# A linear-attention and two-layer MLP kernel: 256-token seven-product form for the second layer's first chunk, states' and score products in array quarters, two warm-up products fewer

## The chip, the core and the metric

One core of a Trainium2 chip runs the whole program. The metric is the time of one execution on the device, in microseconds (us), as the median of several runs; less is better. The core has a matrix engine (PE, with its weight loads listed as PEld), a vector engine (DVE), an activation engine (ACT), a third elementwise engine (POOL), and DMA queues that SP issues here. Matrix products are written to eight banks of an accumulation memory (`ps`), 128 partitions by 512 float32 each.

## What is computed

Linear attention with a decay per head, in blocks of the sequence, and then two MLP layers. Cut to what matters:

```
intra = (q k^T * Dmask) v                        per block, Dmask = lam^(i-j), lower triangle
inter = (q * lam^(pos+1)) state                  the states' product
state = lam^block * state + (k * lam^(rest))^T v
x     = intra + inter                            1536 tokens x 512 (2 batches, 8 heads of 64)
h     = x @ w_in    (512 x 2048);  g = elu(h);           x = g @ w_out    layer 1
h     = x @ w_in2   (512 x 2048);  g = max(h,0) + alpha*min(h,0);  out = g @ w_out2
```

Inputs and results are float32 (the weights float64, read as pairs of words).

## The kernel before

**Precision.** For the MLP each float32 operand is split into a high and a low part (names end in `h` and `l`), and a product of two operands is three matmuls: high x high, high x low, low x high (`for w, x in ((0, 0), (0, 1), (1, 0))`). The attention's products are plain float32; each of their matmuls shows as two records in the trace.

**Attention.** 768 positions are cut into six units of 128, for two batches. A unit has: scores (`scores`, L618: per batch and pair of heads one matmul for each head, on 64 rows of the array, 128 columns of weights), masked by DVE; outputs (`outputs`, L693, on 64-column halves of the array); the update of the state (`state`, L660, 64-column halves; its sum stays in bank 6, is copied to `st` by `new_states`, L412/L414, and decayed in place by ACT, L681); and the states' product (`earlier`, L713: per batch four full 128x128 matmuls with a state tile that has two heads on its diagonal and zeros elsewhere). POOL multiplies keys and queries by powers of the decay (`scale`, L637, L644). Units 0 and 1 make chunk 1 of the tokens (512 of them), 2 and 3 chunk 2, 4 and 5 chunk 0. Key/query blocks (0.5 MB each) and value blocks come through SP's queue in order, four units ahead, then units 4 and 5 behind the first weights.

**MLP.** Each layer has eight steps j; a step handles 256 of the 2048 hidden features as two tiles q. Chunks t = 1 and 2 are taken together: `seven` (L894) forms the four quarter blocks of their up products with seven products in place of eight (a Strassen-like scheme: `PRODUCTS` names the weight part, the token part and the sum that each goes to), six matmuls of 512 columns each. Copies of the bank on ACT (`kept`) and adds on DVE (`tile`, L908) form the other sums between the products; the sums of token blocks (T1 to T4) are made once per layer by `combine` and `combine_parts`, the sums of weights (S1 to S4) each step. Chunk 0, the first chunk, is `plain` (L862): per tile twelve matmuls of 512 columns, four contraction blocks times three. `finish` (L807, L818 to L824, L412, L420) activates a tile out of its bank by way of a buffer `rt` (three in turn) into a buffer `g` (eight in turn, `gfree`), split into high and low. `down` (L959) multiplies two `g` tiles with the down weights, six matmuls per 128 outputs, and DVE adds them to `acc` (L971). Weights are converted from words to float32 by ACT and DVE (L446 to L454) and split.

**What sets the order.** No instruction is issued where the code writes it. `Plan` collects operations with estimated costs, buffers read and written and a latency `LAT`, works out when each is needed, and simulates the engines in several rounds (`ROUNDS`); the best round's order is issued, engine by engine. On PE a change of the array's tiling (`mode`: full, rows, cols) costs `CHANGE` in the plan; `STAY`, `SPARE`, `EASE` and `HOLD` are thresholds of its choices. On the chip each engine then runs its own list in order, and semaphores hold it where an operand is not there.

**The start.** `begin` runs three warm-up matmuls (L602), the small products that spread the decays over partitions, and three more, before the first scores.

Of the kernel before, what the change touches and what calls it, by code (L numbers as in the profile page):

```python
# [15 lines left out]
C = 128  # L16
# [40 lines left out]
class Plan:  # L57
# [5 lines left out]
    SPARE = 5.0  # L63
    EASE = 0.3
    HOLD = 2.0
    ROUNDS = 6
    FETCH = 45.0
    AHEAD = 384.0
    STAY = 2.0
    CHANGE = 0.2  # L70
    ENGINES = ("PE", "SP", "ACT", "DVE", "POOL")
# [48 lines left out]
    def simulate(self, first, back=False, log=None):  # L120
# [11 lines left out]
        stock, seen, mode = self.AHEAD, 0.0, None  # L132
# [12 lines left out]
        def begin(e, op):  # L145
            nonlocal dma, stock, seen, mode
            cost = op.costs[e]
            if e == "PE":
                cost += self.CHANGE * (op.mode != mode)
                mode = op.mode  # L150
# [28 lines left out]
        while done < len(self.ops):  # L179
            for e in self.ENGINES:  # L180
# [12 lines left out]
                while ready[e]:  # L193
# [7 lines left out]
                    if e == "POOL" and any(  # L201
# [4 lines left out]
                        continue  # L206
                    slow = op.costs[e] - op.least
# [8 lines left out]
                for item in held:  # L216
                    heapq.heappush(ready[e], item)
            now = events[0][0]
# [11 lines left out]
    def run(self):  # L230
# [4 lines left out]
        first, best = self.needs(), None  # L235
        for _ in range(self.ROUNDS):
            log = []
            begun, end = self.simulate(first, log=log)
            if best is None or end < best[0]:
                best = end, log  # L240
            begun, end = self.simulate({op: -t for op, t in begun.items()}, True)
            first = {op: -t - op.least - op.late for op, t in begun.items()}
# [21 lines left out]
def attention_two_layers(  # L264
# [27 lines left out]
    warm = sb("warm", [128])  # L292
    anti = sb("anti", [C])
    lams_sb = sb("lams_sb", [H + NP])
    lam_sb, lamp = lams_sb[:, 0:H], lams_sb[:, H:H + NP]
    last_key = sb("last_key", [64])
    row = mem.tile([1, 128 + H], F32, tag="row", name="row")
    fill = sb("fill", [32])

    pair_acc = sb("acc", [2, 4, CH])  # L300
# [20 lines left out]
    rts = sb("rt", [3, CH])  # L321
# [10 lines left out]
    def x0(p):  # L332
        return later_tile(("x0", p), f"x0{'hl'[p]}", [NCC, CH], F32R, f"x0{p}")

# [20 lines left out]
    st = low[:, 2:4].rearrange("p b (a i) -> p b a i", a=NP)  # L355
    top = sb("qpsm", [3, 512], F32, "ut")
    qp = top[:, 0].rearrange("p (a i) -> p a i", a=NP)
    lamc = qp[:, :, C - 1:C]
# [13 lines left out]
    b_quad.update({("T4", p, o): b_quad["B12", p, o] for p in range(2) for o in range(2)})  # L372
    b_x0 = {(p, o): Buf() for p in range(2) for o in range(4)}
# [7 lines left out]
    b_rt = [Buf() for _ in range(3)]  # L381
# [49 lines left out]
    def convert(l, j, part):  # L431
# [16 lines left out]
        op({"DVE": vec2(1024)}, lambda e: nc.vector.tensor_scalar(  # L448
# [75 lines left out]

    late = []

    def combine_parts(o):

        cols = slice(o * 256, (o + 1) * 256)

# [643 lines left out]
```

## Time and profile before

| what | value |
|---|---|
| median of 3 runs | 557.79 us (557.32 to 558.06) |
| the profiled execution | 558.09 us, of which span 556.3 us |
| PE busy | 550.7 us, 99% |
| DVE, POOL, ACT busy | 69%, 58%, 53% |
| HBM read, written | 45.62 MB, 3.15 MB |

How to read it: the profile covers one execution, from its first to its last instruction (the span). An engine is busy while one of its instructions runs; matmuls overlap, so the steps from start to start tell PE's speed, and a matmul's own duration (0.39 us for 512 columns) includes its way through the array. A chain of waits follows the last instruction back to what released it, step by step.

### The profile page before, as it was taken

The page shows a single profiled execution, that of the slowest core. Times are in us where ns is not written, and L with a number is a line of the kernel's source. Part 1 is how long each engine was busy: PE and PEld are TensorE (multiplying, and loading weights), DVE is VectorE, ACT ScalarE, POOL GpSimd, SP SyncE. Part 2 cuts the span into 40 slices and gives each one's busy share as a digit, 9 for nine tenths or more (in the row PEclk, how much of TensorE's full clock was granted, in tenths as well). Part 3 has the DMA queues.
Part 4 walks back from the last instruction along what each step waited for, and adds up shares of the span by engine and source line. Part 5 has one row for each costly group of instructions (what it writes and reads, how often), then busy time and mean ns, then how long its engine had stood idle before and what let it go on. Part 6 is the DMA issues. An engine that isn't in the chain of part 4 may idle for free.

```text
span 556.3 us, 7398 instructions
## 1 busy us (share of the span) xinstructions
PE 550.7 (99%) x2872; PEld 458.3 (82%) x2872; DVE 383.8 (69%) x499; ACT 294.0 (53%) x470; POOL 324.4 (58%) x226
## 2 busy tenths in 40 slices
PE   9999999999999999999999999999999999999997
PEld 7888888888888888888888888888888888888886
DVE  5689688797676757577856964649676757674554
ACT  3586775757475646557645646644454535434220
POOL 4655742556769474928459679477666583927020
DMA  8992222201404222221310120132222222000114
GB/s 326 402 368 80 77 75 77 75 18 59 153 0 152 75 77 75 75 77 49 133 47 1 75 77 1 46 106 77 75 77 75 77 75 77 0 1 0 39 38 151
DMA packets 18308, 49.23 MB, mean 88 GB/s; under 512 B 1250, under 2 KB 1506, under 8 KB 18274
## 3 DMA queue, kind: packets, MB, share of 16 engines
q1 hardware_dynamic: 18272, 48.77, 25.2%
q8 instruction: 22, 0.36, 0.3%
q14 instruction: 12, 0.10, 0.1%
q10 hardware_dynamic: 2, 0.00, 0.0%
HBM read 45.62 MB, written 3.15 MB: 88 GB/s over the span
## 4 chain that ended last, share of the span: by engine, by line
PE 97%; ACT 1%; DVE 1%; issue 0%; ACTq 0%
PE ps L959 47%; PE ps L894 24%; PE ps L862 20%; PE ps L618 2%; PE ps L693 2%; PE ps L713 2%; PE ps L660 1%; PE ps L602 1%; ACT kd L634 0%; ACT dmst L412 0%; DVE dmst L414 0%; DVE qpsm L624 0%; ACT qbh L412 0%; ACT wt L446 0%; ACT ps L681 0%
## 5 line engine op out<-in xcount | busy, mean ns | idle before, releaser
L971 DVE TENSOR_TENSOR acc<-ps,acc 128x512 f32<-128x512 f32 (+1 forms) x169 | 115.9, 687 | 93.1 <-PE ps L959 91.9
L420 POOL TENSOR_TENSOR g<-rt,g 128x512 fp32r<-128x512 f32 x83 | 120.4, 1457 | 80.5 <-ACT g L412 78.2
L959 PE MATMUL ps<-wdh,g 128*128 128x512 f32 (+1 forms) x388 | 118.4, 387 | 0.0
L959 PE MATMUL ps<-g,wdh 128*128 128x512 f32 x384 | 118.1, 389 | 0.0
L807 ACT ACTIVATE rt<-ps 128x512 f32<-128x512 f32 x96 | 57.3, 598 | 95.7 <-DVE ps L908 55.9
L959 PEld LDWEIGHTS ps<-wdh,g 128*128 128x128 f32 x388 | 72.6, 188 | 14.9
L959 PEld LDWEIGHTS ps<-g,wdh 128*128 128x128 f32 x384 | 72.1, 188 | 14.9
L412 ACT CAST g<-rt 128x512 fp32r<-128x512 f32 x96 | 59.3, 620 | 38.9 <-DVE rt L824 25.2
L959 PE MATMUL ps<-wdl,g 128*128 128x512 f32 (+1 forms) x194 | 75.0, 387 | 0.0
L959 PE MATMUL ps<-g,wdl 128*128 128x512 f32 x192 | 74.7, 389 | 0.0
L420 POOL TENSOR_TENSOR wsl<-wt,wsh 128x1024 fp32r<-128x1024 f32 x12 | 29.4, 2449 | 47.8 <-ACT wsh L412 29.9
L824 DVE SCALAR_TENSOR_TENSOR rt<-rt,beta,ps 128x512 f32<-128x512 f32 x48 | 35.6, 742 | 25.9 <-ACT rt L807 25.9
L420 POOL TENSOR_TENSOR wt<-wt 128x256 f32<-128x256 f32 x54 | 42.4, 796 | 12.5 <-DVE wt L454 5.9
L420 POOL TENSOR_TENSOR wdl<-wt,wdh 128x1024 fp32r<-128x1024 f32 x14 | 38.1, 2723 | 19.5 <-ACT wdh L412 19.3
L454 DVE SCALAR_TENSOR_TENSOR wt<-raw,wt 128x1024 uint32<-128x1024 uint32 x32 | 46.0, 1436 | 0.0
L908 DVE TENSOR_TENSOR ps<-ps,ut 128x512 f32<-128x512 f32 x42 | 29.3, 698 | 21.9 <-PE ps L894 21.8
L959 PEld LDWEIGHTS ps<-wdl,g 128*128 128x128 f32 x194 | 36.4, 188 | 7.4
L412 ACT COPY ut<-ps 128x512 f32<-128x512 f32 x42 | 24.6, 589 | 33.5 <-PE ps L894 33.4
L959 PEld LDWEIGHTS ps<-g,wdl 128*128 128x128 f32 x192 | 36.0, 188 | 7.6
L451 DVE SCALAR_TENSOR_TENSOR wt<-raw,wt 128x1024 uint32<-128x1024 uint32 x32 | 42.0, 1316 | 0.2
L446 ACT ACTIVATE wt<-raw 128x1024 f32<-128x1024 f32 x32 | 36.6, 1143 | 4.7 <-POOL wt L420 3.1
L862 PE MATMUL ps<-x0l,wah 128*128 128x512 f32 x128 | 38.8, 389 | 0.0
(127 smaller groups left out, 932.9 us busy)
## 6 DMA issues: line engine op xcount, KB each, us to landing
raw<-in_w1i SPq DMA_DIRECT2D x8, 1024.0 KB, 5.5
raw<-in_w1o SPq DMA_DIRECT2D x8, 1024.0 KB, 4.9
raw<-in_w2i SPq DMA_DIRECT2D x8, 1024.0 KB, 5.6
raw<-in_w2o SPq DMA_DIRECT2D x8, 1024.0 KB, 4.8
blk<-in_kqT SPq DMA_DIRECT2D x12, 512.0 KB, 11.5
blk<-in_vk SPq DMA_DIRECT2D x10, 512.0 KB, 11.5
out<-acc SPq DMA_DIRECT2D x11, 256.0 KB, 2.0
blk<-in_vk SPq DMA_DIRECT2D x2, 256.0 KB, 9.4
```

Source lines behind the costliest of these rows:

```text
L412: nc.scalar.copy(dst(), src())
L420: lambda e: on(e).tensor_tensor(out=dst(), in0=a(), in1=b(), op=alu),
L446: op({"ACT": 1.14}, lambda e: nc.scalar.mul(t, upper.bitcast(F32), 2.0 ** -112), [b_r], [b_t])
L451: op({"DVE": vec(1024)}, lambda e: nc.vector.scalar_tensor_tensor(out=tu, in0=lower, scalar=29, in1=tu, op0=ALU.logical_shift_right, op1=A ...
L454: op({"DVE": vec(1024)}, lambda e: nc.vector.scalar_tensor_tensor(out=tu, in0=upper, scalar=0x80000000, in1=tu, op0=ALU.bitwise_and, op1=A ...
L807: op({"ACT": act(512, True)}, lambda e: nc.scalar.activation(rt(i), h(), AF.Relu, scale=-1.0), [b_h], [b_r])
L824: op({"DVE": vec(512) + 0.06}, lambda e: nc.vector.scalar_tensor_tensor(out=rt(i), in0=rt(i), scalar=beta[:, f:f + 1], in1=h(), op0=ALU.mu ...
L862: nc.tensor.matmul(out=banks[k], lhsT=wa(s, w)[:, cc, q * 128:(q + 1) * 128], rhs=(both[t][x] if t else x0(x))[:, cc, :], start=i == 0, st ...
L894: nc.tensor.matmul(out=banks[k], lhsT=left(s, a, w)[:, cc, :], rhs=quad(b, x)[:, cc, :], start=bool(opens and i == 0), stop=bool(closes an ...
L908: op({"DVE": vec(512)}, lambda e: nc.vector.tensor_tensor(out=banks[to], in0=banks[k], in1=ut(u), op=ALU.add), [b_ps[k], b_ut[u]], [b_ps[to]])
L959: nc.tensor.matmul(out=p_, lhsT=lhs, rhs=rhs, start=i == 0, stop=i == 5)
L971: op({"DVE": vec(w)}, lambda _, a=a, p_=p_: nc.vector.tensor_tensor(out=a(), in0=p_, in1=a(), op=ALU.add), [b_ps[k], *b_a], b_a)
```

## The change

- **First chunk, second layer.** From step j = 2 on (`FIRST = [8, 2]`: never in the first layer) the up products of chunk 0 are made by `seven_halves`: its 512 tokens are two halves of 256, which take the places of chunks 1 and 2 in the seven-product scheme, with six matmuls of 256 columns per product. The four sums share two banks by halves. `combine_halves` makes the sums T1 to T4 of the halves once, at the beginning of the layer; they live in two former `g` buffers and a new one, so `gfree` has six, and `rt` two.
- **Quarters.** Scores and states' product run on 64x64 quarters of the array. The state holds 64x64 blocks without the zeros, for batch 1 with the two halves of the partitions exchanged (`rows`), so that one product of 16 matmuls serves both batches, alternating over the quarters. The queries of batch 1 are multiplied in two halves, to exchange them; DVE may do it too. The state is copied in one piece, and decayed per batch and pair with a power from a small copy (`last`).
- **Warm-up.** One matmul in place of three behind the decays' products.
- **Plan.** Other thresholds, four rounds, doubled PE costs in the first 6.5 us, higher costs of the weight conversion's DVE steps.

```diff
-    SPARE = 5.0
-    EASE = 0.3
-    HOLD = 2.0
-    ROUNDS = 6
+    ROUNDS = 4
...
+    RULES = [(4.0, 5.0, 0.3, -1.0)]
...
-    rts = sb("rt", [3, CH])
+    rts = sb("rt", [RT, CH])
...
+        if m in ("T1", "T2", "T3"):
+            i = int(m[1])
+            tag = f"g{5 + i}" if i < 3 else "qh3"
+            return later_tile(("qh", i), "qh", [2, 2, CH // 2], F32R, tag)[:, p]
+        c, o = {"B11": (0, 0), "B21": (1, 0), "B22": (1, 1), "T4": (0, 1), "B12": (0, 1)}[m]
+        return x0(p)[:, 2 * c:2 * c + 2, o * 256:(o + 1) * 256]
...
+            self.rows = [half(hs ^ b) for hs in range(2)]
...
                 for pr in range(NP):
-                    for hs in range(2):
+                    for hs, s in ((0, 0), (1, 1), (0, 1), (1, 0)):
                         nc.tensor.matmul(
-                            out=banks[ks[hs]][:, pr * C:(pr + 1) * C],
-                            lhsT=x.kq[half(hs), 0, pr, :], rhs=x.kq[half(hs), 1, pr, :],
-                            start=True, stop=True)
-            pe(0.89, run, [x.b_kq], [b_ps[k] for k in ks], 32, "rows")
+                            out=banks[ks[hs]][half(s), pr * C:(pr + 1) * C],
+                            lhsT=x.kq[half(hs), 0, pr, half(s)],
+                            rhs=x.kq[half(hs), 1, pr, :], start=True, stop=True)
+            pe(0.86, run, [x.b_kq], [b_ps[k] for k in ks], 64, "quarters")
...
+            pe(0.86, run, [b_st, *b_qs[m % 2]], [b_ps[k] for k in ks], 64, "quarters")
...
-        plan.behind(pe(0.4, spread, [b_row, b_one], [b_ps[k]]), run_up(3))
+        plan.behind(pe(0.4, spread, [b_row, b_one], [b_ps[k]]), run_up(1))
...
-    gfree = [4, 5, 6, 7, 0, 1, 2, 3]
+    gfree = [4, 5, 0, 1, 2, 3]
...
+    def seven_halves(l, j):
+        s = j % 2
+        ka, kb = 3 + j % 2, 4 - j % 2
+        left_, right_ = slice(0, 256), slice(256, 512)
+        home = {0: (kb, left_), 1: (ka, left_), 2: (ka, right_), 3: (kb, right_)}
...
+                        nc.tensor.matmul(
+                            out=at(k), lhsT=left(s, a, w)[:, cc, :], rhs=halved(b, x)[:, cc, :],
...
+            def kept(u, k=k):
+                copy(lambda: ut(u)[:, left_], lambda: at(k), [b_p[k]], [b_ut[u]], 256, True)
...
+            if b == "B11":
+                kept(0)
+            elif b == "B21":
+                tile(0, 1)
+            elif b == "T1":
+                kept(1)
+            elif b == "T2":
+                kept(2)
+            elif b == "B22":
+                tile(2, 2)
+                finish(l, 2 * j, lambda: banks[ka], [b_p[1], b_p[2]], (l, j, 0, 0), True)
+            elif b == "T3":
+                tile(1, 3)
+            else:
+                finish(l, 2 * j + 1, lambda: banks[kb], [b_p[0], b_p[3]], (l, j, 1, 0), True)
...
             else:
+                combine_halves(1)
                 merge((), downs(1, 0, T0))
...
-                            plain(l, j + 1)),
+                            first(l, j + 1)),
```

The new states' product, with the loops that set the order of the quarters:

```python
for pr in range(NP):
    for hs in range(2):
        for b, x in enumerate(units[m]):
            nc.tensor.matmul(
                out=banks[ks[b]][half(hs), pr * C:(pr + 1) * C],
                lhsT=st[x.rows[hs], b, pr, :],
                rhs=qss[m % 2][x.rows[hs], b, pr * C:(pr + 1) * C],
                start=False, stop=True, skip_group_check=True)
```

What moves on PE around the end of the attention, from the states' product of unit 3 on. Before (L618 scores, L713 states' product, L693 outputs, L660 state, L862 the first up product, tile by tile):

```order
L618 MATMUL ps<-blk 128x128 x8
L713 MATMUL ps<-qs,dmst 128x128 x4
L693 MATMUL ps<-sm,blk 64x128 x8
L618 MATMUL ps<-blk 128x128 x8
L862 MATMUL ps<-qbh,wah 128x512 x4
L862 MATMUL ps<-qbl,wah 128x512 x4
L862 MATMUL ps<-qbh,wal 128x512 x4
L660 MATMUL ps<-blk,kd 64x64 x16
L693 MATMUL ps<-sm,blk 64x128 x8
L618 MATMUL ps<-blk 128x128 x8
L713 MATMUL ps<-qs,dmst 128x128 x8
```

And of the change (L671 scores, L768 states' product, L748 outputs, L721 state, L927 up product):

```order
L671 MATMUL ps<-blk 64x128 x32
L768 MATMUL ps<-qs,dmst 64x128 x16
L671 MATMUL ps<-blk 64x128 x32
L927 MATMUL ps<-qbh,wah 128x512 x4
L927 MATMUL ps<-qbl,wah 128x512 x4
L927 MATMUL ps<-qbh,wal 128x512 x4
L748 MATMUL ps<-sm,blk 64x128 x16
L721 MATMUL ps<-blk,kd 64x64 x16
L768 MATMUL ps<-qs,dmst 64x128 x16
```

Both batches' scores of unit 5 now stand ahead of the first up product (before, those of its second batch stood behind it), and both batches' states' product of unit 4 is one group.

The first chunk's up products in the second layer, on PE, before (`ps_80` and `ps_81` are banks 3 and 4, `ps_82` to `ps_84` the banks of the down products):

```order
L862 MATMUL ps_80<-x0h_108,wah_503 128x512 x4
L862 MATMUL ps_80<-x0l_109,wah_503 128x512 x2
L959 MATMUL ps_82<-wdh_589,g3_845 128x512 x2
L959 MATMUL ps_82<-wdl_599,g3_845 128x512
L959 MATMUL ps_82<-wdh_589,g0_727 128x512 x2
L959 MATMUL ps_82<-wdl_599,g0_727 128x512
L862 MATMUL ps_80<-x0l_109,wah_503 128x512 x2
L862 MATMUL ps_80<-x0h_108,wal_516 128x512 x4
```

And of the change, at step j = 6 (`ps_78` and `ps_79` are banks 3 and 4; `qh_2375`, `qh_2425` and `qh_2414` hold T1, T2 and T3 of the halves):

```order
L1013 MATMUL ps_78<-qh_2375,wsh_933 128x256 x4
L1013 MATMUL ps_78<-qh_2375,wsl_1006 128x256 x2
L1013 MATMUL ps_79<-qh_2425,wsh_933 128x256 x4
L1013 MATMUL ps_79<-qh_2425,wsl_1006 128x256 x2
L1013 MATMUL ps_78<-x0h_106,wsh_933 128x256 x2
L1013 MATMUL ps_78<-x0l_107,wsh_933 128x256 x2
L1013 MATMUL ps_78<-x0h_106,wsl_1006 128x256 x2
L1013 MATMUL ps_79<-qh_2414,wsh_933 128x256 x4
L1013 MATMUL ps_79<-qh_2414,wsl_1006 128x256 x2
```

Four products of 256 columns follow each other directly; the third adds to the bank half that the first wrote, the fourth to that of the second, and a copy by ACT (`kept`) reads each half in between.

## Rows read from the trace of the kernel before

**Rows 1.** The page: busy time by engine, and the chain that ended last, by engine.

```profile
PE 550.7 (99%) x2872; PEld 458.3 (82%) x2872; DVE 383.8 (69%) x499; ACT 294.0 (53%) x470; POOL 324.4 (58%) x226
...
PE 97%; ACT 1%; DVE 1%; issue 0%; ACTq 0%
```

**Rows 2.** Stretches: us; busy PE, PEld, DVE, ACT, POOL; granted clock, DMA share, GB/s.

```profile
27.80:40.48 12.68, 11.88 (x190) 10.60 (x189) 10.15 (x13) 11.13 (x26) 6.06 (x5) 1.00 1.00 377
...
54.93:553.20 498.27, 498.27 (x2205) 412.43 (x2203) 342.83 (x438) 260.84 (x394) 294.62 (x197) 1.00 0.19 65
```

**Rows 3.** The chain in order of time: start, us, what; one first chunk (L862).

```profile
102.81 5.44 PE ps L862 x24
```

**Rows 4.** Timeline of PE and weight loads at the end, 256 columns: start, us, instruction.

```profile
551.62 0.40 PE L959 MATMUL ps<-wdh,g 128*128 128x256 f32 x2
...
552.58 0.31 PEld L959 LDWEIGHTS ps<-wdh,g 128*128 128x128 f32 x2
...
552.93 0.28 PE L959 MATMUL ps<-wdl,g 128*128 128x256 f32 x1
```

**Rows 5.** Timeline of PE in the attention.

```profile
3.59 1.65 PE L602 MATMUL ps<-warm 128*128 128x128 f32 x6
5.17 3.79 PE L618 MATMUL ps<-blk 64*128 64x128 f32 x32
...
23.38 2.06 PE L618 MATMUL ps<-blk 64*128 64x128 f32 x32
25.37 1.97 PE L693 MATMUL ps<-sm,blk 128*64 128x128 f32 x32
27.27 2.05 PE L713 MATMUL ps<-qs,dmst 128*128 128x128 f32 x16
29.25 1.15 PE L660 MATMUL ps<-blk,kd 128*64 128x64 f32 x32
30.23 1.05 PE L693 MATMUL ps<-qpsm,blk 128*64 128x128 f32 x16
...
40.48 1.19 PE L862 MATMUL ps<-qbh,wah 128*128 128x512 f32 x4
...
43.44 1.15 PE L660 MATMUL ps<-blk,kd 128*64 128x64 f32 x32
...
45.40 1.16 PE L618 MATMUL ps<-blk 64*128 64x128 f32 x16
46.49 2.05 PE L713 MATMUL ps<-qs,dmst 128*128 128x128 f32 x16
48.30 1.18 PE L862 MATMUL ps<-qbh,wah 128*128 128x512 f32 x4
...
51.23 1.09 PE L693 MATMUL ps<-qpsm,blk 128*64 128x128 f32 x16
...
53.13 2.05 PE L713 MATMUL ps<-qs,dmst 128*128 128x128 f32 x16
54.93 1.17 PE L862 MATMUL ps<-qbh,wah 128*128 128x512 f32 x4
```

**Rows 6.** Timeline of POOL and DVE there: unit 5's queries, the up weights' low part.

```profile
38.07 3.51 POOL L644 TENSOR_TENSOR qs<-blk,qpsm 128x512 f32<-128x512 f32 x2 [0.22 <-DMA blk<-in_kqT]
...
38.95 1.48 DVE L420 TENSOR_TENSOR wal<-wt,wah 128x1024 fp32r<-128x1024 f32 x1
```

**Rows 7.** Timeline in the second layer: a product's end on PE and its copy on ACT.

```profile
431.49 0.62 PE L894 MATMUL ps<-qT2h,wsl 128*128 128x512 f32 x2
...
432.14 0.59 ACT L412 COPY ut<-ps 128x512 f32<-128x512 f32 x1 [1.61 <-PE ps L894]
```

**Rows 8.** Groups by line and shape on ACT: count, busy us, mean ns, idle before.

```profile
L446 ACT ACTIVATE wt<-raw 128x1024 f32<-128x1024 f32 x32 | 36.6, 1143 | 4.7 <-POOL wt L420 3.1 <-DMA raw<-in_w2i 0.8 <-DMA raw<-in_w1o 0.4
...
L412 ACT COPY ut<-ps 128x512 f32<-128x512 f32 x42 | 24.6, 589 | 33.5 <-PE ps L894 33.4
...
L783 ACT ACTIVATE qpsm<-ps,lams_sb 128x128 f32<-128x128 f32 x4 | 1.1, 369 | 7.3 <-PE ps L787 7.3
```

More of the change, by code (lines that the diff above doesn't have):

```diff
@@ L148, in begin @@
             if e == "PE":
+                if now < self.COLD and not back:
+                    cost *= 2
                 cost += self.CHANGE * (op.mode != mode)
@@ L234, in run @@
                 a.before.append(op)
[L235 to L242, printed above, removed]
+        best = None
+        for self.STAY, self.SPARE, self.EASE, self.HOLD in self.RULES:
+            first = self.needs()
+            for _ in range(self.ROUNDS):
+                log = []
+                begun, end = self.simulate(first, log=log)
+                if best is None or end < best[0]:
+                    best = end, log
+                begun, end = self.simulate({op: -t for op, t in begun.items()}, True)
+                first = {op: -t - op.least - op.late for op, t in begun.items()}
         for e, op in best[1]:
@@ L291, in attention_two_layers @@
     beta = sb("beta", [2 * NU])
-    warm = sb("warm", [128])
-    anti = sb("anti", [C])
+    early = sb("early", [2, CH], F32, "qh3").rearrange("p a b -> p (a b)")
+    warm, anti = early[:, 0:128], early[:, 128:256]
+    last_key, fill = early[:, 256:320], early[:, 320:352]
+    row = early[0:1, 384:512 + H]
     lams_sb = sb("lams_sb", [H + NP])
[L295 to L298, printed above, removed]
+    lam_sb, lamp = lams_sb[:, 0:H], lams_sb[:, H:]
+    last = [sb(f"last{b}", [NP]) for b in range(B)]
+    RT = 2
     pair_acc = sb("acc", [2, 4, CH])
@@ L380, in attention_two_layers @@
     b_ut = [Buf() for _ in range(3)]
-    b_rt = [Buf() for _ in range(3)]
+    b_rt = [Buf() for _ in range(RT)]
     b_ps = [Buf() for _ in range(8)]
@@ L779, in masks @@
                     data1=anti, initial=0.0, op0=ALU.mult, op1=ALU.add)
-        def powers(e):
-            for pr in range(NP):
-                nc.scalar.mul(qp[:, pr], p2[:, pr * C:(pr + 1) * C], lamp[:, pr:pr + 1])
+        for hs in range(2):
+            op({"DVE": 1.3}, lambda e, hs=hs: masks(e, hs), [b_lam, b_anti], [b_dm[hs]], True)
+        k = turn("ps", 8)
+        p2 = banks[k]
         def last_row():
@@ L984, in merge @@
         while True:
+            while not gfree and next(dn, None):
+                pass
             a, b = next(up, None), next(dn, None)
```

237 lines of the change are left out of this document (155 added, 82 removed).

## The prediction

> **What bounds the kernel.** I read the page's shares first, then the chain of waits, then the stretches, then the timeline of PE. PE is busy 99% of the span and carries 97% of the chain that ended last [rows 1]; DVE at 69% and ACT at 53% hold 1% of it each, POOL at 58% nothing. The stretches divide the span in two. From 54.93 to 553.20 us PE is busy for all of 498.27 us [rows 2]. A 512-column product takes 5.44 / 24 = 0.2267 us there [rows 3]; of the kernel's 2214 such matmuls 24 stand ahead of 54.93, and 2190 x 0.2267 + 12 x 0.12 (the narrow ones at the end) = 497.9 us. That is the stretch, so nothing stalls in it, and only fewer or faster matmuls, or a new stall, change its length. Ahead of it lies the attention. Up to 40.48 us the DMA engines are full (share 1.00, 377 GB/s [rows 2]), and POOL waits for key and query blocks as they land: the first of unit 5 at 38.07 [rows 6]. So there two limits lie close together.
>
> **Part 1: the first chunk's up products in the second layer.** A chunk was 24 matmuls of 512 columns, 5.44 us [rows 3]. It becomes seven products of six matmuls of 256 columns. The trace has that width at its end: from 551.62 to 552.93 lie 11 steps, 0.119 us each; the weight loads, 0.31 us for two that overlap, run without a gap beside them [rows 4]. So 42 x 0.12 = 5.04 us, 0.40 us less. The loop takes this form for j = 2 to 7, six chunks: **-2.4 us**. Where PE is the bound throughout, this counts in full, if the order causes no stall.
>
> What it adds elsewhere: per chunk three ACT copies and three DVE adds of 256 columns, and once four sums and four splits of the chunk (16 operations of DVE, POOL and ACT). The new halves are first read after the whole second j = 1 stage; DVE, POOL and ACT have 31, 42 and 47% of the span free for them [rows 1]. I cost them at nothing; were their cover gone, the 12 subtractions among them are the largest part.
>
> The wait it adds: products pass through ACT copies before the same half bank is added to again. In the order eight times only one product of 0.72 us (6 x 0.12) stands between. What has to fit: in the trace a product's last issue at 431.49 + 0.45 ends its slot at 431.94, and the copy starts at 432.14, 0.20 later [rows 7]. A 256-column copy lies between 369 ns (128 columns) and 589 ns (512) [rows 8], 0.44 by a straight line. With 0.05 for the way back that is 0.69 against 0.72. So the wait is nil if ACT is free, and up to 1.14 us if a weight conversion (1143 ns [rows 8]) has just begun; behind the waiting matmul all of PE is queued. ACT is idle about half the time [rows 1], so I am near the lower end: 0.1 us each, **+0.8 us** (bounds 0 and 8 x 1.14 = 9.1).
>
> Two resources shrink: six buffers for activated tiles instead of eight, two for results in work instead of three. In PE's new order the shortest time from a buffer's last reader to its next is five products, 5 x 6 x 0.2267 = 6.8 us (before: nine, 12.2), and it must hold a cast and a split. I cost both at nothing; a stall would fall on PE at full price.
>
> **Part 2: the attention in quarters.** A record of the state product in two column tiles costs (30.23 - 29.25) / 32 = 0.0306 us; two score products of 16 records cost 1.99, a single one between other modes 45.40 to 46.49 = 1.09 [rows 5]. So a second block costs 0.90, and changing the array's mode 0.19. No row shows a quarter tile. If four run at once, a product of 32 records costs no less than 0.98 (the fastest record there is); if only two do, 32 x 0.0563 = 1.80. Both halves, rows (scores) and columns (states), do show two at once, so I take 0.98. Then a states' product of both batches falls from 1.80 (46.49 to 48.30 [rows 5]) to 0.98, five times; a score block goes from 0.90 to 0.98, twelve times, the first unit's two at the slow rate of the start.
>
> What lies on the path? PE's order puts both score blocks of unit 5 ahead of the first up product. At 377 GB/s a block of 0.52 MB takes 1.4 us, so their second key block lands near 39.4, its scores end near 40.4, and the first up product starts where it did, at 40.48. The weights for it are no earlier bound (their last DVE step ended at 38.95 + 1.48 = 40.43 [rows 6]). From there the trace needs 14.45 us to 54.93 [rows 5]. After: up 2.96 (40.48 to 43.44), outputs 1.90, state 0.98, states' product 0.98 + 0.17 for the change, up 2.93 (48.30 to 51.23), outputs 1.90, states' product 1.15 = 12.97. **-1.5 us.** Ahead of 40.48 about 3.3 us of PE work go as well (three states' products -2.5, nine changes of mode -1.7, four warm-up records -1.05, the moved score block +1.0, slower scores 11 x 0.08 = +0.9); they turn into waiting for unit 5. The two warm-up matmuls are 4 of the 6 records of 1.58 us [rows 5], all inside this slack; that the scores then start earlier and still at the slow rate (3.79 / 32 = 0.118 us a record, against 0.062 in the later pair [rows 5]) costs nothing there. Bounds of the part: +1.6 if two tiles run at once in the two late states' products alone, and 1.3 us more gain if the last key block lands with the first.
>
> The queries' products become 15 for 10, 13 on POOL, at up to 3.51 / 2 = 1.76 us each [rows 6]; the last reader, unit 5's states' product, stands 11.8 us behind the first up product, so they are hidden. The state is copied in one piece for two, and ACT's three small copies run once, at the start. I cost these at nothing.
>
> A rule of the Trainium skill speaks against this part: the page TensorEngine Tiling (Array Packing), section Restrictions and Gotchas, says that different row tiles can't use one PSUM bank at the same time. In the new states' product each batch has one bank, and both row halves write it. The scores' pair at 1.99 us [rows 5] shows two row tiles at once on separate banks; no run here shows them on one. By the rule the product would run two tiles at a time, and the sum be 556.3 in place of 554.7; it is the first rival.
>
> **Sum.** -2.4 + 0.8 - 1.5 = -3.1 us on the profiled execution's 558.09 us (span 556.3 and 1.8 around it) = 555.0; that execution lies 0.3 above the median 557.79, so the forecast is **554.7 us** on the median's scale. What a measurement can tell here is about 0.2%, 1.1 us.
>
> **Rivals.** *One bank, two tiles* (11%): states' products cost 1.80. The three early ones (+2.5) still fit into the 3.3 us of slack; the two late ones take back 2 x 0.82. 557.79 - 2.4 + 0.8 - 1.5 + 1.6 = 556.3. For it: no row shows otherwise; against it: different partitions of the bank are written.
> *The short cover in the halves* (16%): each of the eight waits meets half a weight conversion, 0.57 us, or the fewer buffers stall PE as much. +4.6 for +0.8: 558.5. For it: conversions stand right ahead of some of these copies in ACT's order; against: ACT follows PE without one stall now. The part breaks even at 0.3 us a wait.
> *Quarters run two at a time everywhere* (8%), the slower side: ten later score blocks +8.2 (0.82 each), the first unit's +3.6 (64 records at 0.118 for 32), states' products +4.1, less the 3.3 of slack and the 1.5: +11.1 in place of -1.5, so 557.79 - 2.4 + 0.8 + 11.1 = 567.3. It decides from 0.041 us a record on, where 620 records (the slow ones counted by their price) use up the slack and both gains. For it: no row of quarters; against: each half already gives the factor two, and weight loads of two tiles overlap.
> *The last key block lands early* (13%): attention 1.3 better and no waits in the halves: 552.6.
> That the halves don't run at 0.12 would need 0.13 a matmul to lose the gain; with rows 4 I give it no chance of its own.
>
> **How the numbers follow.** Forecast 52%, with its own range 553.3 to 556.2. Faster by over 0.2% (under 556.7): forecast 51, early block 13, one bank 7, a little of the short cover 1: 0.72. Slower (over 558.9): quarters 8 and a quarter of the short cover 4: 0.12. The rest, 0.16, is no change. The range goes down to 552.0, under the early block, and up to 558.6, past the short cover's time; beyond lie the quarters above and little below.
>
> **What would show it.** The halves: 42 matmuls of 256 columns per chunk at 0.12 steps, and PE idle ahead of them, released by the copy on ACT: 0.8 us in all if I am right, over 3 if the short cover holds. Quarters: 32 records of scores in 0.98 us after the first unit, and of states in 0.98 (1.80 by the rule on banks). Waiting of PE between 36 and 40 us that ends with scores of unit 5; first up product near 40.5, the unbroken stretch from about 53.4. Wrong would be a stall of PE in the first layer or at the change of layers, or an up product that starts well ahead of 40 us.

## The result: 0.9% slower

The changed kernel takes **562.64 us** (median of 5 runs, 562.1 to 563.14) against 557.75 us of the kernel before, run beside it: ratio 1.0087, 95% interval 1.0073 to 1.0100. I had predicted 554.7 us, in a range of 552.0 to 558.6. Of the 7.9 us between forecast and time, nearly all was lost in the first 80 us, where the prediction had costed new things at nothing.

### The profile page after: what moved, and what is told of

It reads as the page before. It is cut to its first block, busy times and chain, and to the rows that moved or that the text cites. A ratio compares the mean times of both kernels' runs of the same rounds, so it can differ in the third digit from the quotient of the medians.

```text
span 560.7 us, 8291 instructions
## 1 busy us (share of the span) xinstructions
PE 546.8 (98%) x3248; PEld 458.5 (82%) x3248; DVE 427.2 (76%) x565; ACT 305.3 (54%) x530; POOL 277.6 (50%) x187
## 4 chain that ended last, share of the span: by engine, by line
PE 92%; ACT 3%; DVE 2%; DMA 1%; issue 1%; SPq 0%; ACTq 0%
PE ps L1086 47%; PE ps L959 24%; PE ps L927 12%; PE ps L1013 5%; PE ps L748 2%; DMA blk<-in_kqT 1%; PE ps L671 1%; ACT ps L736 1%; PE ps L721 1%; PE ps L768 1%; ACT kd L687 1%; DVE ut L438 0%; ACT qbh L430 0%; DVE g L438 0%; SPq L418 0%
## 5 line engine op out<-in xcount | busy, mean ns | idle before, releaser
L1098 DVE TENSOR_TENSOR acc<-ps,acc 128x512 f32<-128x512 f32 (+1 forms) x169 | 115.0, 684 | 63.0 <-PE ps L1086 61.6
L438 POOL TENSOR_TENSOR g<-rt,g 128x512 fp32r<-128x512 f32 x62 | 91.3, 1473 | 102.9 <-ACT g L430 92.2
L1086 PE MATMUL ps<-g,wdh 128*128 128x512 f32 x384 | 118.6, 390 | 2.8 <-DVE acc L432 2.8
L1086 PE MATMUL ps<-wdh,g 128*128 128x512 f32 (+1 forms) x388 | 118.9, 388 | 0.0
L1086 PEld LDWEIGHTS ps<-g,wdh 128*128 128x128 f32 x384 | 72.2, 188 | 18.2 <-DVE acc L432 3.2
L1086 PEld LDWEIGHTS ps<-wdh,g 128*128 128x128 f32 x388 | 71.6, 188 | 14.2 <-DVE acc L1098 0.3
L1086 PE MATMUL ps<-wdl,g 128*128 128x512 f32 (+1 forms) x194 | 75.1, 387 | 0.0
L1086 PE MATMUL ps<-g,wdl 128*128 128x512 f32 x192 | 74.9, 390 | 0.0
L430 ACT COPY ut<-ps 128x512 f32<-128x512 f32 (+1 forms) x60 | 31.4, 523 | 63.4 <-PE ps L959 44.6
L438 POOL TENSOR_TENSOR wal<-wt,wah 128x1024 fp32r<-128x1024 f32 x13 | 31.3, 2405 | 49.8 <-ACT wah L430 39.2
L884 DVE SCALAR_TENSOR_TENSOR rt<-rt,ps 128x512 f32<-128x512 f32 x48 | 32.2, 682 | 16.6 <-ACT rt L882 15.9
L1086 PEld LDWEIGHTS ps<-wdl,g 128*128 128x128 f32 x194 | 36.4, 188 | 7.6
L1086 PEld LDWEIGHTS ps<-g,wdl 128*128 128x128 f32 x192 | 36.1, 188 | 7.5
L438 POOL TENSOR_TENSOR wsl<-wt,wsh 128x1024 fp32r<-128x1024 f32 x12 | 34.3, 2856 | 15.7 <-ACT wsh L430 11.5
L438 POOL TENSOR_TENSOR wt<-wt 128x256 f32<-128x256 f32 x42 | 34.2, 831 | 13.5 <-DVE wdl L438 8.9
L438 DVE TENSOR_TENSOR g<-rt,g 128x512 fp32r<-128x512 f32 x34 | 37.4, 1108 | 4.5 <-ACT g L430 4.1
L438 POOL TENSOR_TENSOR wdl<-wt,wdh 128x1024 fp32r<-128x1024 f32 x10 | 24.7, 2472 | 31.7 <-ACT wdh L430 31.6
```

The source lines that it names most:

```text
L430: nc.scalar.copy(dst(), src())
L438: lambda e: on(e).tensor_tensor(out=dst(), in0=a(), in1=b(), op=alu),
L884: op({"DVE": vec(512)}, lambda e: nc.vector.scalar_tensor_tensor(out=rt(i), in0=rt(i), scalar=-1.0, in1=h(), op0=ALU.add, op1=ALU.max), [b ...
L1086: nc.tensor.matmul(out=p_, lhsT=lhs, rhs=rhs, start=i == 0, stop=i == 5)
L1098: op({"DVE": vec(w)}, lambda _, a=a, p_=p_: nc.vector.tensor_tensor(out=a(), in0=p_, in1=a(), op=ALU.add), [b_ps[k], *b_a], b_a)
```

## The profile after

First the page: busy time, the granted clock in 40 slices, the transfers of instructions, and the chain by engine.

```profile
span 560.7 us, 8291 instructions
PE 546.8 (98%) x3248; PEld 458.5 (82%) x3248; DVE 427.2 (76%) x565; ACT 305.3 (54%) x530; POOL 277.6 (50%) x187
...
PEclk8989989999999999999999999999999999999999
...
q8 instruction: 25, 0.41, 0.3%
...
PE 92%; ACT 3%; DVE 2%; DMA 1%; issue 1%; SPq 0%; ACTq 0%
```

PE has 3.9 us less to do than before [rows 1], and yet the span is 4.4 us longer (556.3 before): PE now idles, and in three of the first six slices its granted clock shows 8 tenths and not 9. "issue" holds 1% of the chain, where it held 0 [rows 1]. Second, PE's waits: engine, line, what released it, us in total, times, longest.

```profile
PE ps L1086 <- DVE acc L432: 2.8, 1, 2.8
PE ps L748 <- DVE qbl L787: 2.1, 2, 1.4
PE ps L671 <- DMA blk<-in_kqT: 2.0, 1, 2.0
PE ps L721 <- issue: 1.3, 1, 1.3
...
PE ps L721 <- ACT ps L736: 1.0, 1, 1.0
```

None of them is in the kernel before. Third, PE's timeline in the attention, which answers to [rows 5].

```profile
10.62 1.99 PE L671 MATMUL ps<-blk 64*64 64x128 f32 x32 [1.96 <-DMA blk<-in_kqT]
12.54 2.66 PE L748 MATMUL ps<-sm,blk 128*64 128x128 f32 x32
...
19.96 1.15 PE L721 MATMUL ps<-blk,kd 128*64 128x64 f32 x32 [1.05 <-ACT ps L736]
...
21.92 1.10 PE L671 MATMUL ps<-blk 64*64 64x128 f32 x32
...
27.59 0.45 PE L721 MATMUL ps<-blk,kd 128*64 128x64 f32 x7
29.38 0.92 PE L721 MATMUL ps<-blk,kd 128*64 128x64 f32 x25 [1.34 <-issue]
...
34.57 1.98 PE L748 MATMUL ps<-sm,blk 128*64 128x128 f32 x16 [0.70 <-DVE qbl L787]
...
43.40 1.20 PE L927 MATMUL ps<-qbh,wah 128*128 128x512 f32 x4
...
55.33 1.10 PE L768 MATMUL ps<-qs,dmst 64*64 64x128 f32 x32
56.36 1.20 PE L927 MATMUL ps<-qbh,wah 128*128 128x512 f32 x4
```

The reader is to see three things. A quarter product does what I took (0.98 us): 32 records from 21.92 to the next at 22.84, 0.92 us, and 55.33 to 56.36, 1.03 us, for the states' product, on one PSUM bank a batch. From the first up product to the third it is 56.36 - 43.40 = 12.96 us, where I had worked out 12.97. But the first up product stands at 43.40 and not at 40.48: PE had idled at 8.67 (1.96 us), 18.92 (1.05), 28.04 (1.34), 31.33 (1.44) and 33.87 (0.70). And behind some of these gaps matmuls take twice as long: the same 32 scores 1.99 us at 10.62 and 1.10 at 21.92.

Fourth, stretches: us; busy PE, PEld, DVE, ACT, POOL; granted clock, DMA share, GB/s.

```profile
8.67:17.60 8.93, 6.97 (x136) 6.50 (x140) 3.79 (x7) 6.18 (x24) 5.91 (x5) 0.81 1.02 413
29.38:43.40 14.02, 11.71 (x281) 10.46 (x280) 11.09 (x14) 9.77 (x29) 6.20 (x4) 0.88 0.84 309
...
71.62:78.78 7.16, 4.41 (x13) 3.46 (x13) 6.82 (x8) 2.28 (x5) 1.55 (x1) 0.77 0.00 0
```

What was one unbroken stretch [rows 2] now has a hole at 71.62, in the first layer; on both sides of it PE is busy throughout. The granted clock is below 1.00 in these three stretches, which each hold a gap: a mean of its two levels (1.2 and 2.4 GHz). Fifth, what stands around the hole on PE, DVE and POOL.

```profile
74.37 0.73 PE L1086 MATMUL ps<-g,wdh 128*128 128x512 f32 x2 [2.75 <-DVE acc L432]
...
76.22 1.91 PE L927 MATMUL ps<-x0h,wah 128*128 128x512 f32 x4
...
67.55 3.40 DVE L438 TENSOR_TENSOR g<-rt,g 128x512 fp32r<-128x512 f32 x2 [0.26 <-ACT g L430]
70.87 2.84 DVE L438 TENSOR_TENSOR ut<-ut 128x512 f32<-128x512 f32 x1
73.64 0.68 DVE L432 COPY acc<-ps 128x512 f32<-128x512 f32 x1
...
67.40 1.30 POOL L438 TENSOR_TENSOR qT3l<-ut,qT3h 128x512 fp32r<-128x512 f32 x1
68.78 1.62 POOL L438 TENSOR_TENSOR ut<-qbh,qbl 128x512 f32<-128x512 f32 x1
70.36 2.81 POOL L438 TENSOR_TENSOR wsl<-wt,wsh 128x1024 fp32r<-128x1024 f32 x1
```

PE waits for a copy of the accumulator, because the next down product goes to the same bank (in both kernels the first step's products of chunks 1 and 2 have one bank, `FILL = [7]`). The product that it copies had ended at 70.1; the copy stands on DVE behind two splits and a subtraction, of 0.68 us each when alone. They took 1.70, 1.70 and 2.84: each ends about 0.5 us after the POOL instruction beside it has ended (68.70, 70.40, 73.17). In the kernel before, the same copy starts 0.2 us behind its product (68.65), with DVE idle just ahead of it:

```profile
68.85 0.69 DVE L414 COPY acc<-ps 128x512 f32<-128x512 f32 x1 [0.36 <-PE ps L959]
```
Four up matmuls behind the hole take 1.91 us where four took 1.07.

In spans: third up product 56.36 for 54.93, **+1.4**; the hole 2.75 and the slow matmuls behind it (74.37 to 78.78 for 2.72 us of work, 1.69), **+4.4**; halves and the rest of the second layer **-1.8**; small things +0.4. That is the 4.4 of the span.

## The experiments

Each was timed beside the kernel before; the ratio is to it, with its 95% interval. A trace is one execution, and executions differ: the changed kernel, copy_early and first_plain have the same attention, and their first up products start at 43.40, 44.03 and 42.46.

| run | us, median | ratio |
|---|---|---|
| the changed kernel | 562.64 | 1.0087 [1.0073, 1.0100] |
| copy_early | 558.98 | 1.0021 [1.0008, 1.0033] |
| decay_four | 563.32 | 1.0097 [1.0080, 1.0114] |
| warm_three | 561.79 | 1.0078 [1.0056, 1.0100] |
| first_plain | 564.99 | 1.0125 [1.0110, 1.0140] |
| rows_scores | 555.32 | 0.9952 [0.9937, 0.9967] |
| halves_new | 556.52 | 0.9973 [0.9963, 0.9983] |
| halves_old | 560.03 | 1.0036 [1.0023, 1.0049] |
| best_b | 555.77 | 0.9954 [0.9938, 0.9971] |
| before_quarters | 557.82 | 1.0001 [0.9992, 1.0011] |
| rows_decay | 556.15 | 0.9980 [0.9969, 0.9991] |
| tuned | 554.07 | 0.9941 [0.9924, 0.9958] |
| rows_split | 569.76 | 1.0201 [1.0181, 1.0222] |

**copy_early: is the hole one engine's queue?** In the planner's list, operation 201 (the copy) is put ahead of 278 (the subtraction):

```diff
+        log.insert(at, log.pop(to))   # at: 278, to: 201, both DVE's
         for e, op in log:
             op.run(e)
```

> The changed kernel's trace has PE idle for 2.75 us at 71.62 and then at the lower clock for some 3.4 us; DVE's copy that it waits for stands behind two splits and a subtraction that ran 1.70, 1.70 and 2.84 us beside POOL's. Here that one copy goes ahead of the subtraction in DVE's order, all else in the order stays. Theory A (a queue on one engine): the 2.75 us go and with them the slow matmuls behind (another 1.7), 558.2 in place of 562.64. Rival B (that copy is only the first of several late things): the wait moves to the next product, less than 1.5 us come back, 561.1 or more.

3.7 us faster: theory A, less what came back. Another 0.8 us wait, for ACT's copy of the next product, took its place, so part of B is true as well:

```profile
76.10 0.74 PE L1091 MATMUL ps<-g,wdh 128*128 128x512 f32 x2 [0.80 <-ACT acc L435]
```

No matmul behind it was slow any more. So the place of the copy in DVE's list makes the hole. That POOL lengthened the operations ahead of it is read from the trace; no run took POOL's work away.

**decay_four: was it the decay?** The change made the decay eight instructions on ACT; the prediction had overlooked that.

```diff
-                for b in range(B):
-                    for pr in range(NP):
-                        nc.scalar.mul(view[:, b, pr, :], view[:, b, pr, :], last[b][:, pr:pr + 1])
+                for pr in range(NP):
+                    nc.scalar.mul(view[:, :, pr, :], view[:, :, pr, :], last[0][:, pr:pr + 1])
```

> Leaves out the second batch's own decay: both batches of the state are scaled by the first batch's powers, in four instructions on ACT in place of eight, the order of everything else unchanged. The eight took 2.52 us in the changed kernel. Theory A (the decay on ACT stands in the chain of the attention; its doubling, which the prediction did not count, is a good part of the lost 2.9 us ahead of the first up product): each decay about 1.1 us shorter, PE's idle time from 17.66 to 19.96 about 1.1 us shorter, first up product 1 to 2.5 us ahead of 43.40, total 560 to 561.6. Rival B (the DMA's or another chain sets the pace): first up product within 0.4 us of 43.4, total 562.2 to 562.9.

No gain: the decay is 1.45 us now (2.52 before the edit), PE's wait at 18.92 is gone (the expectation dates it from 17.66; the wait itself is the 1.05 us before 19.96), and the first up product comes at 43.08, 0.3 earlier, which is less than executions differ by. (The total doesn't price the decay: a new wait of 1.2 us for a result in work stands ahead of the third up product.) The trace (ACT's decay, then PE) shows what took the place of the wait:

```profile
17.57 1.45 ACT L735 ACTIVATE ps<-ps,last 128x128 f32<-128x128 f32 x4
...
21.96 0.49 PE L767 MATMUL ps<-qs,dmst 64*64 64x128 f32 x9
23.67 0.77 PE L767 MATMUL ps<-qs,dmst 64*64 64x128 f32 x20 [1.22 <-issue]
```

PE stops in the middle of a product, with nothing named that it waits for. That led to the theory of the instruction supply: that PE stops because its next instructions have not been fetched.

**warm_three: were the warm-up matmuls free?** `for _ in range(n)` becomes `for _ in range(3)` in the group.

> The second group of warm-up matmuls again three long, two more than in the changed kernel, the order of everything else unchanged. Theory A (the removed warm-up is inside slack, as predicted): first up product within 0.3 us of 43.40 and the total within 0.4 of 562.64. Rival B (the earlier start only opens an idle stretch of PE, 8.67 to 10.62, after which the clock falls): that stretch shrinks from 1.96 to about 0.9 us, the matmuls of the second unit run at the full rate (32 records of scores in 1.0 and not 1.99 us), and 1 to 2 us come back: 560.6 to 561.6.

0.85 us faster by the medians, though the executions overlap (561.31 to 563.44, and 562.10 to 563.14 of the changed kernel); first up product at 42.55 and not 43.40. As B has it, the gap at 8.67 is gone and the second unit's scores take 1.10 us, at a granted clock of 1.00 to 17.60; less came back than B says. But first_plain's trace (below), with one warm-up matmul as in the changed kernel, has no such gap either: its second unit's scores start at 9.83 without a wait and take 1.11 us, and its first up product stands at 42.46. So the gap comes and goes between executions, and what the warm-up matmuls are worth is not shown. The stops of PE in the middle of a product are there too, at other records. PE's timeline in this run:

```profile
21.16 0.40 PE L768 MATMUL ps<-qs,dmst 64*64 64x128 f32 x5
21.89 0.98 PE L768 MATMUL ps<-qs,dmst 64*64 64x128 f32 x26 [0.33 <-issue]
...
26.45 0.29 PE L721 MATMUL ps<-blk,kd 128*64 128x64 f32 x3
28.45 1.04 PE L721 MATMUL ps<-blk,kd 128*64 128x64 f32 x29 [1.71 <-issue]
```

And in the run with the copy put ahead:

```profile
21.09 0.49 PE L773 MATMUL ps<-qs,dmst 64*64 64x128 f32 x9
23.34 0.77 PE L773 MATMUL ps<-qs,dmst 64*64 64x128 f32 x20 [1.77 <-issue]
...
27.84 0.45 PE L726 MATMUL ps<-blk,kd 128*64 128x64 f32 x7
29.62 0.92 PE L726 MATMUL ps<-blk,kd 128*64 128x64 f32 x25 [1.34 <-issue]
```

There PE stops after 9 records of the one product and after 7 of the other, as in decay_four (9) and the changed kernel (7). warm_three has four more records ahead, from two warm-up matmuls, and stops after 5 and 3: four earlier in both. Counted from the program's start, the two stops lie behind 347 and 473 matmul records in each of these traces (the changed kernel has the second alone, first_plain both, and copy_early a short one behind 220 as well). So they lie at fixed counts of PE's instructions, not at a time or an operand; and 126 or 127 records with a weight load each are 252 or 254 instructions, near the 260 that come to one instruction transfer over the whole trace (6,496 in 25). In the changed kernel a transfer of 16 KB on the instruction queue lies in 26:27 us, just ahead of its stop at 28.04 (the queue's row of that one microsecond):

```profile
q8 instruction: 1, 0.02, 6.8%
```

**first_plain: are the halves worth it?** `FIRST = [8, 2]` becomes `[8, 8]`, which keeps the old form of the first chunk. (The halves' sums are still written over that chunk, so its products run on other numbers.)

> The second layer's first chunks in their old form, 24 matmuls of 512 columns, in all else the changed kernel; the order up to the second layer is the same. Theory A (the halves give what was predicted, 6 x 0.40 us less a wait here and there): slower than the changed kernel by 1.6 to 2.4 us, 564.2 to 565.0, and all of it behind 264 us. Rival B (short cover or fewer buffers eat the gain): within 0.5 us of 562.64 or faster.

2.35 us slower, as theory A has it. But 0.8 of it is a wait that only this trace has, at the change of layers (`PE ps L1086 <- DVE acc L1098`), so the edit's own worth is nearer 1.6. The changed kernel's trace shows why it is not the 2.6 that its rows of 256 columns (0.119 a step) would give:

```profile
429.28 0.40 PE L1013 MATMUL ps<-qh,wsl 128*128 128x256 f32 x2
429.52 0.63 PE L1086 MATMUL ps<-wdh,g 128*128 128x512 f32 x2
...
430.91 0.40 PE L1013 MATMUL ps<-x0h,wsh 128*128 128x256 f32 x2
```

Six matmuls of 512 columns behind a group of halves take 1.39 us (429.52 to 430.91), not 1.36; over all such groups of the trace 0.7 us. No wait stands here: PE's idle time at L1013 is nil.

**rows_scores: the scores in rows again**, on top of copy_early, in the same order.

```diff
-                    for hs, s in ((0, 0), (1, 1), (0, 1), (1, 0)):
-                        nc.tensor.matmul(
-                            out=banks[ks[hs]][half(s), pr * C:(pr + 1) * C],
-                            lhsT=x.kq[half(hs), 0, pr, half(s)],
-                            rhs=x.kq[half(hs), 1, pr, :], start=True, stop=True)
+                    for hs in range(2):
+                        nc.tensor.matmul(
+                            out=banks[ks[hs]][:, pr * C:(pr + 1) * C],
+                            lhsT=x.kq[half(hs), 0, pr, :], rhs=x.kq[half(hs), 1, pr, :],
+                            start=True, stop=True)
```

> As the run with the copy put ahead (558.98 us), and in it the score products in the form of before, 16 matmuls of two row tiles a block in place of 32 quarters, in the same order. In that run three waits of PE named issue, 1.8, 1.3 and 0.3 us, each end 1.1 to 1.5 us after an instruction transfer of 16 KB has ended; in the kernel before there is none. Theory A (twice as many matmuls eat up PE's instructions faster than they come while the DMA engines are full): with 192 fewer matmul records ahead of the first up product the issue waits fall under 0.7 us in sum, the first up product comes 1.5 to 3 us ahead of 44.03, and the total is 556 to 557.7. Rival B (the waits are put down wrongly, the chain through ACT and DVE sets the pace): the same time is lost elsewhere, total 558.4 to 559.4.

3.7 us faster than copy_early and 0.5% faster than the kernel before; theory A, and more. In copy_early three waits were put down to issue, 3.4 us in all:

```profile
PE ps L773 <- issue: 1.8, 1, 1.8
...
PE ps L726 <- issue: 1.3, 1, 1.3
...
PE ps L676 <- issue: 0.3, 1, 0.3
```

In rows_scores there is none, and the first up product starts 4.4 us earlier (39.61 for 44.03; 2.9 before the earliest trace of the same attention, 42.46), though its score blocks take as long (2.06 us for two, 1.98 in quarters). The lower clock is gone too: 0.87 in copy_early from 30.47 to 44.03, 1.00 in rows_scores over the same products (27.09 to 39.61). So the 3.7 us are the stops and the clock together. Its waits:

```profile
PE ps L752 <- DVE qbl L791: 2.1, 2, 1.4
...
PE ps L725 <- ACT ps L740: 1.4, 2, 1.0
...
PE ps L1090 <- ACT acc L434: 0.8, 1, 0.8
```

**halves_new and halves_old: the attention of before**, first with the planner's new constants, then also with the old ones (`STAY` 2, `HOLD` 2, six rounds, no slow start, the old costs of the conversion).

> The halves of the second layer, the fewer buffers and the new constants of the planner kept; the attention as in the kernel before (three warm-up matmuls, rows, columns, state in two copies, four decays). Theory A (quarters and what belongs to them cost all that was lost): 557.75 less 2.35 for the halves, 555.0 to 555.9, first up product near 40.5, no stall in the first layer. Rival B (the planner's new constants make an order that stalls, whatever the attention): idle time of PE over 1.5 us between 56 and 110 us and 557 us or more.

> As the run with the attention of before, and the planner's constants of before too: only the halves and the buffers that they need (two for results in work, six for activated tiles) are new. Theory A: 555.0 to 555.9, as with the new constants. Rival B (the new constants are at fault): this one 555.4 and the other one 557 or more. Rival C (the fewer buffers stall the first layer): both 557 or more, PE waiting for a split or a result in work there.

556.52 and 560.03: the first is nearer to A (though its first up product, at 41.42, is 0.9 us later than A has it), the pair the reverse of B. With the new constants there is no hole, only two small waits, and the halves bring 1.5 of their 2.35 us. With the old constants the order puts short waits in front of the halves, the ones that I had priced at 0.1 us each (the second run's waits of PE):

```profile
PE ps L1010 <- ACT ut L431: 0.6, 2, 0.3
PE ps L1010 <- DVE ps L1026: 0.4, 2, 0.2
```

Its third up product also comes 0.7 us later than the other's (55.48 for 54.80); behind it the second run is 2.2 us longer, of which its waits are 1.2. So the new constants are not the cause of the hole, and whether the halves wait depends on the order.

**before_quarters: only the score quarters, in the kernel before** (rows_scores' edit the other way round).

> The kernel before, with one edit: the score products in quarters, 32 matmuls of a quarter each in place of 16 of two row tiles, in the same order. Theory A (instruction supply): PE now waits for issue for 1 us or more between 15 and 40 us, which it never does in the kernel before, each wait ending a little over 1 us behind an instruction transfer; first up product 41 to 43.5 us in place of 40.48, total 558.3 to 561. Rival B (quarters only cost their own time, 0.08 us a block, and the DMA-bound stretch swallows it): first up product within 0.5 us of 40.48, total 557.4 to 558.4, no issue wait over 0.4 us.

Rival B: 557.82, no issue wait at all, first up product at 40.00. So theory A missed: the quarters in the scores don't starve PE by themselves. The five traces with both scores and states' products in quarters show the stops; with one of the two (this run, rows_scores) or neither (halves_new) there is none, though the orders differ as well. Why it takes both is not shown. With the states' products in four big matmuls a batch there are stretches of few instructions between the scores; but this run fetches seven 16 KB transfers in its first 60 us, as many as the changed kernel, so the mean rate is not the difference.

**rows_split: as many instructions, no quarters.** Each row score is cut into two matmuls of 64 moving columns.

> The run with the scores in rows (555.32 us, no issue wait), and in it every score matmul cut in two along its moving columns: 32 matmuls a block as with quarters, but on two whole row tiles and with the same columns streamed; the order is the same. Theory A (it is the number of instructions, not the place of the quarters in the array): issue waits of PE come back at the same records as with quarters (7 of the 32 of the fourth unit's state product, 9 of a states' product), 1 to 4 us in sum; 557 to 559.5. Rival B (quarters on one bank or their mode is at fault): no issue wait over 0.4 us, 555 to 556.3.

Neither: 569.76 us, 10 us above both theories, with the first up product at 53.32. 64 such records took 3.79 us where 32 of 128 columns take 2.06, 0.059 us each for 0.064, so the score instructions came at about half the rate of quarters, and there was no issue wait. It doesn't contradict the supply theory and doesn't test the count apart from the rate.

**rows_decay: the decay again, now with rows_scores.**

> The run with the scores in rows (555.32 us), and in it the decay in four instructions with the first batch's powers for both batches (the second batch's own decay is left out). In the changed kernel that edit gave nothing, since an issue wait came in place of the decay's. Theory A (with the supply no longer short, the decay is the next in the chain): the two waits of PE for the decay (0.96 and 0.43 us) go, first up product about 1 us ahead of 39.61, total 553.9 to 554.7. Rival B (the key blocks or the copies of the outputs are next, close behind): less than 0.4 us, 554.9 to 555.5.

Rival B, and worse: the first up product stays (39.62), since PE then waits 1.4 us for the last key block, in this line's own row:

```profile
37.23 2.46 PE L675 MATMUL ps<-blk 64*128 64x128 f32 x32 [1.42 <-DMA blk<-in_kqT]
39.62 1.21 PE L930 MATMUL ps<-qbh,wah 128*128 128x512 f32 x4
```

So the loads do set a floor near 39.6, as I had argued for 40.48; the runs with quarters in scores and states' products don't reach it. Behind it a new wait of 1.2 us for a result in work made the time worse.

**best_b and tuned: what the findings are worth.** The first, put together anew by the planner, has the decay in one DVE instruction; the second is rows_scores with five moves in the lists of ACT and DVE and three warm-up matmuls:

```diff
+        for n, m in [(201, 199), (203, 202), (279, 203), (35, 122), (36, 123)]:   # n goes right behind m
+            at = {op.n: i for i, (e, op) in enumerate(log)}
+            x = log.pop(at[n])
+            log.insert(at[m] + (at[m] < at[n]), x)
```

> A version put together from the findings: halves; states' products in quarters, scores in rows as before; three warm-up matmuls; the decay in one instruction on DVE (512 elements, 0.68 us) in place of eight on ACT (2.52); the planner's constants of before but for the slow start. If the instruction supply and the decay were what held the attention up, the first up product comes at 39.5 to 41 us, the two late states' products give their 1.5 us, and the total is 553 to 555 us, under both kernels. If the order stalls somewhere in the first layer as the changed kernel's does, 556 to 558.

> The run with the scores in rows (555.32 us) with the small waits that its trace names taken away: three warm-up matmuls again; on ACT and DVE the second output copy ahead of a weight conversion; on ACT the accumulator's copy ahead of the cast that waits for DVE's subtraction. By the waits: 0.84 us and about 0.3 of slow matmuls behind it in the first layer, 0.6 at the output copy, up to 0.9 by the warm-up if nothing else is late, so 553.2 to 554.4. If the waits only move on, 554.8 to 555.6.

555.77 and **554.07 us**. best_b, between its two forecasts, lost what it won to an order with a 2.6 us wait for the decay. tuned, in its range, has no wait in the layers left, granted clock 1.00 throughout, and starts the third up product at 52.46, 2.5 us ahead of the kernel before. It beats both kernels, 0.6% under the one before.

## Why the prediction was wrong

- **Part 1, -2.4 + 0.8.** The size is right, 1.6 to 1.8 us, but by luck: no wait for ACT in the changed kernel (priced at 0.8), and in its place 0.7 us of slower 512-column matmuls behind the halves, which I had not thought of. The waits that I priced appear in other orders (halves_old, best_b).
- **"I cost both at nothing; a stall would fall on PE at full price."** This step failed: I had put a stall in the first layer at nothing, and it cost 4.4 us, of which copy_early gets 3.7 back. That the fewer buffers are the reason was not shown: halves_new has them too and no such hole. What was shown is the queue: a copy behind three DVE operations, which ran long beside POOL's. I had looked at the distance between a buffer's users on PE, and not at what DVE's list holds ahead of the copies that free PE's banks. My own test ("Wrong would be a stall of PE in the first layer") found it.
- **"... the first up product starts where it did, at 40.48", with 3.3 us of PE work that "turn into waiting for unit 5".** This failed too, by 2.9 us. PE lost more than this slack ahead of 43.40, to stops and to the lower clock: in the changed kernel's trace the five gaps hold 6.5 us (1.96 for keys, 1.05 for the decay, 2.14 for the copies of the outputs, 1.34 for issue), and the lower clock behind them costs some 3.1; in copy_early's the stops for issue are 3.4 and the lower clock 1.5. rows_scores, with 192 matmul records fewer, still waits for keys, decay and copies, but has no stop for issue and a clock of 1.00, and is 3.7 us faster. I had counted records and their time, and not that the count itself may matter: 736 matmul records of the attention, for 496, up to the first up product. That instructions came too late is the reading which the fixed counts favour; before_quarters and rows_split, meant to confirm it, did not.
- **The two warm-up matmuls, "all inside this slack".** Not shown wrong: the 0.85 us of warm_three lie within what executions differ by, and first_plain has no gap at 8.67 with one warm-up matmul.
- **The queries, the copies.** I overlooked that the decay went from four instructions to eight. PE waits for it at 18.92 (1.05 us), but with four the first up product comes no earlier than in other traces of this attention.
- **From the first up product on, 12.97 us.** Right (12.96), though the terms miss by up to 0.13 either way, a wait of 0.18 ahead of the second up product among them.
- **Rivals.** One bank, two tiles: refuted; a states' product of 32 records took 1.03 us. By the Trainium skill, page TensorEngine Tiling (Array Packing), section Restrictions and Gotchas, row tiles can't use one bank at the same time; the measurement differs, and decides. Quarters two at a time: refuted, so my slower side was the wrong mechanism (and its +3.6 for the first unit should be 32 x 0.118 = 3.8). Early key block: half right (floor 39.6), hidden in the changed kernel by what PE lost ahead of it. The short cover: not here.

The sum adds up: 557.75 - 2.35 (halves) + 3.66 (562.64 - 558.98, the copy) + 3.66 (558.98 - 555.32, the quarters in the scores) = 562.7. That it does so within 0.1 us is partly luck: 0.8 of the 2.35 is first_plain's own wait, and with 1.6 for the halves the sum is 0.8 over. All else of the change, the 1.5 us of the late states' products among it, must then net to something between nothing and a gain of 0.8. Open is what made the planner put the copy there, how far ahead of its need a 16 KB transfer is asked for, and why the clock falls behind the same gaps in one execution and not in another.

## What to carry over

Slack on the bounding engine ahead of a fixed time is only slack if the engine can be fed: count its instructions as well as its time, and see whether "issue" waits come at fixed counts. Before a difference of 1 us between two traces is given a cause, look at a third trace of the same stretch. When an order is made anew, look at each copy that frees a bank, and at what stands ahead of it in its engine's list; DVE work on two SBUF inputs there must be priced with POOL's beside it. And an idle gap costs more than its length if the clock falls behind it.

## What the hardware showed that I had not expected

- **Instruction supply (read from counts, not proved).** Stops of 0.3 to 1.8 us, most in the middle of a product, at fixed instruction counts. The trace has 6,496 matmuls and weight loads on PE and 25 transfers of 16 KB. The Trainium skill, page Runtime: NRT & Kernel Launch, section Instruction fetch mechanics, says that instructions come in blocks of 16 KiB (256 instructions), and that the cost of crossing a block's end is mostly hidden. The count agrees; hidden it is in the layers, where a matmul takes 0.2267 us, and, if the stops are what I take them for, not in an attention of 0.03 us records with the DMA engines full (413 GB/s from 8.67 to 17.60).
- **DVE behind POOL.** 0.68 us operations took 1.70 and 2.84, each ending about 0.5 us after POOL's. The Trainium skill, page SBUF — State Buffer, section Who interferes with whom, says that a DVE instruction with two SBUF inputs contends with a POOL instruction that reads SBUF, and calls their shared ports an exclusive lock; the trace agrees.
- **The clock.** Behind PE's gaps at 8.67 (1.96 us), 31.33 (1.44 and 0.70 with a product between) and 71.62 (2.75) the granted clock fell to the lower level for a while; behind those at 18.92 (1.05) and 28.04 (1.34) it did not. The three cost about 1.6, 1.5 and 1.7 us, against the same matmuls at full clock in copy_early, decay_four and the layers. The same gaps did not always bring it down: in rows_scores the gap for the second unit's keys (1.85) and the pair of 1.44 and 0.70 left it at 1.00.
- **Narrow matmuls.** Half the moving columns (64) on two row tiles saved almost nothing: 0.059 us each, against 2.06 / 32 = 0.064 with 128 [rows 5].
